# Three of the second product's seven products made by the seven-product scheme once more, from the third unit on

## The chip, the cores and the metric

The kernel runs on one core of a Trainium2 chip. The metric is the device time of one execution in microseconds (us). Where a kernel was compared closely, it was timed in turns with the kernel before on the same chip. TensorE multiplies, VectorE does elementwise work and empties PSUM (the memory, in banks, into which the matmuls add up), ScalarE does activations and copies, and DMA queues move data between DRAM and SBUF (the memory from which the engines take their operands). The granted clock is the share of TensorE's full speed that the profile records.

## The reference, cut to what matters

```python
kv  = np.einsum('bhsd,bhse->bhde', k, v)          # linear attention: (8, 8, 576, 64)
out = np.einsum('bhsd,bhde->bhse', q, kv)
x   = out / sqrt(mean(out*out, -1) + 1e-6) * g_norm   # then (4608, 512)
h   = x @ w_in                                    # 512 -> 2048   "first product"
g   = s * maximum(h, 0)**2 + b
return g @ w_out                                  # 2048 -> 512   "second product"
```

Everything is fp32.

## The kernel before

The 4608 rows are taken in nine units of 512. From the second unit on, the first and the second product of a unit are each made by a Strassen-Winograd scheme: seven products of half-sized blocks in place of eight. For the second product one of the seven is 256 rows x 1024 x 256; it runs as two row halves `j`, each eight matmuls of 128x128 by 128x256. The products are made in the order 1, 2, 6, 7, 5, 3, 4. Products 1, 6, 5 and 3 add up in one PSUM bank per half, and 7 and 4 in another. VectorE reads the bank between them.

```python
def product(i, j, ps, first):
    w2 = W2_AT[i] if u == 0 else ring[u, i]        # operand of w_out, a 1 MB tile fetched from DRAM
    for f in range(FC // 2):                       # 8 matmuls, contraction 128 each
        s, b = divmod(f, 2)
        matmul(ps, ga[G_OF[i], s][:, b, j*P : j*P+P], w2[:, f, :],
               first and f == 0, f == FC // 2 - 1)

def scaled(o, ps, other):                          # VectorE: o = s * ps + other, an "eviction"
    nc.vector.scalar_tensor_tensor(o, ps, s_col, other, ALU.mult, ALU.add)

return [lambda: x1(0), seq(lambda: x1(1), nxt(2), s2),   # s2: a11 = s1 - a11, operand of product 6
        lambda: z2(0), seq(lambda: z2(1), nxt(3), s4),   # s4: a12 = a12 - a11, operand of product 3
        lambda: x6(0), ...                               # (cut)
```

Between these steps stands the attention of the next unit's four chunks, by step number (`side`): `turn` transposes q on VectorE, `product` multiplies on TensorE and then squares (ScalarE), reduces and normalises (VectorE), `turn_x` transposes the result on VectorE, and ScalarE then scales it in pairs. The order is fixed by hand: in the traces below VectorE and ScalarE run their instructions in the order in which the program writes them (on VectorE of the changed kernel an eviction at 417.70, four subtractions from 418.10, the next eviction at 420.50; on ScalarE of e4 a scaling that waited 5.33 us at 437.66, and only then a square at 439.27).

## Time and profile before

| | before |
|---|---|
| time, median of the first 3 runs | 972.84 us (972.73 to 973.84) |
| span of the profiled run | 970.5 us |
| TensorE / VectorE / ScalarE busy | 99% / 50% / 20% |
| one unit | 104 us, of which 56.6 us second product |
| granted TensorE clock, mean | 0.998 |

Busy time is the union of an engine's instructions. A matmul record's duration is a model and longer than the spacing of two records (381 ns against 216 ns for 256 columns), so costs are read from start to start. The lines themselves stand in the prediction.

### The profile page before, as it was taken

To read this page: it belongs to the slowest core of one execution; us is meant where nothing else is said; L and a number is where in the kernel's file an instruction comes from. 1 tells how busy PE (TensorE), PEld (TensorE's weight loads), DVE (VectorE), ACT (ScalarE), POOL (GpSimd) and SP (SyncE) were. 2 spreads that over 40 slices of the span, in tenths; PEclk is the share of its full clock that TensorE was granted. 3 is DMA by queue.
4 is the path that set the end of the run, shared out by engine and by line. 5 is a ranking of instruction groups with operands and counts; after the bars stand their busy time and mean duration, and the time that the engine had idled before them with its cause. 6 is when DMAs were issued, how large, how long until landed. Compare 5 with 4: busy or idle time off the path is not lost.

```text
span 970.5 us, 15215 instructions
## 1 busy us (share of the span) xinstructions
PE 958.3 (99%) x6430; PEld 832.7 (86%) x6430; DVE 488.7 (50%) x803; ACT 194.6 (20%) x366; POOL 6.7 (1%) x18
## 2 busy tenths in 40 slices
PE   7999999999999999999999999999999999999997
PEld 7888888888888888888888888888888888888886
DVE  2789766554445434544446434644455345444431
ACT  3673132112120112111211112011201111111100
POOL 2000000000000000000000000000000000000000
PEclk9999999999999999999999999999999999999999
DMA  9588737732463257132363256225213430422032
GB/s 255 192 296 248 247 88 205 164 107 88 130 129 125 87 146 154 58 133 69 94 154 131 74 132 154 87 96 146 64 44 131 134 85 23 151 66 109 1 130 86
DMA packets 106931, 121.59 MB, mean 125 GB/s; under 512 B 74352, under 2 KB 80752, under 8 KB 99568
## 3 DMA queue, kind: packets, MB, share of 16 engines
q1 hardware_dynamic: 103760, 118.85, 41.8%
q10 hardware_dynamic: 2784, 1.77, 0.8%
q8 instruction: 50, 0.82, 0.4%
q14 instruction: 17, 0.14, 0.0%
q0 software_dynamic: 320, 0.00, 0.0%
HBM read 103.81 MB, written 16.78 MB: 124 GB/s over the span
## 4 chain that ended last, share of the span: by engine, by line
PE 95%; DMA 2%; DVE 1%; ACT 1%; SPq 0%; issue 0%; ACTq 0%; DVEq 0%
PE x_ps L87 50%; PE y_ps L87 31%; PE z_ps L87 9%; PE x_ps L412 3%; PE kv_ps L350 2%; DMA w_raw<-in_moe_w_in_dram 1%; DMA kv_sb<-in_k_dram 1%; DMA w_sb<-w 1%; PE qT_ps L391 0%; DVE xn L431 0%; DVE xT L455 0%; ACT xT L461 0%; ACT w_raw L206 0%; SPq L649 0%; DVE o L630 0%
## 5 line engine op out<-in xcount | busy, mean ns | idle before, releaser
L87 PE MATMUL x_ps<-w_sb,a 128*128 128x256 f32 x768 | 172.4, 381 | 0.0
L87 PEld LDWEIGHTS x_ps<-w_sb,a 128*128 128x128 f32 x768 | 145.0, 190 | 21.7 <-issue 2.8
L87 PE MATMUL y_ps<-w_sb,a 128*128 128x256 f32 x640 | 142.9, 381 | 1.4 <-DMA w_sb<-w 1.4
L87 PEld LDWEIGHTS y_ps<-w_sb,a 128*128 128x128 f32 x640 | 121.0, 190 | 19.1 <-DMA w_sb<-w 1.8
L87 PE MATMUL x_ps<-xs,ws 128*128 128x256 f32 x512 | 121.0, 379 | 0.0
L87 PE MATMUL y_ps<-xs,wb 128*128 128x256 f32 x512 | 121.0, 379 | 0.0
L557 ACT COPY r<-x_ps 128x512 f32<-128x512 f32 x96 | 56.2, 585 | 295.7 <-PE x_ps L87 289.0
L87 PEld LDWEIGHTS y_ps<-xs,wb 128*128 128x128 f32 x512 | 97.4, 190 | 13.1
L87 PEld LDWEIGHTS x_ps<-xs,ws 128*128 128x128 f32 x512 | 97.4, 190 | 13.1
L226 DVE TENSOR_TENSOR a<-y_ps,r 128x512 f32<-128x512 f32 x64 | 43.9, 686 | 122.3 <-ACT r L557 122.3
L87 PE MATMUL x_ps<-xT,wa 128*128 128x256 f32 x384 | 89.6, 380 | 0.1
L87 PEld LDWEIGHTS x_ps<-xT,wa 128*128 128x128 f32 x384 | 72.9, 190 | 10.4 <-ACT xT L461 0.5
L514 DVE SCALAR_TENSOR_TENSOR a<-a 128x512 f32<-128x512 f32 x96 | 66.4, 692 | 3.3
L630 DVE SCALAR_TENSOR_TENSOR or<-x_ps,s_col,b_row 128x256 f32<-128x256 f32 x52 | 25.0, 482 | 75.1 <-PE x_ps L87 73.2
L87 PE MATMUL x_ps<-xT,ws 128*128 128x256 f32 x256 | 61.1, 382 | 0.0
L87 PE MATMUL z_ps<-xT,wa 128*128 128x256 f32 x256 | 60.5, 379 | 0.0
L590 DVE TENSOR_TENSOR a<-a 128x512 f32<-128x512 f32 x32 | 22.1, 692 | 76.0 <-ACT a L589 76.0
L421 ACT ACTIVATE xn<-x_ps 128x512 f32<-128x512 f32 x34 | 20.3, 597 | 190.2 <-PE x_ps L412 187.8
L87 PE MATMUL x_ps<-w_sb,s 128*128 128x256 f32 x256 | 57.3, 382 | 0.0
L87 PEld LDWEIGHTS x_ps<-w_sb,s 128*128 128x128 f32 x256 | 48.1, 190 | 7.6 <-issue 1.4
L87 PEld LDWEIGHTS z_ps<-xT,wa 128*128 128x128 f32 x256 | 48.7, 190 | 6.6
L87 PEld LDWEIGHTS x_ps<-xT,ws 128*128 128x128 f32 x256 | 48.2, 190 | 6.6
(106 smaller groups left out, 821.1 us busy)
## 6 DMA issues: line engine op xcount, KB each, us to landing
w_sb<-w SPq DMA_DIRECT2D x56, 1024.0 KB, 5.0
kv_sb<-in_k_dram SPq DMA_DIRECT2D x30, 288.0 KB, 4.9
kv_sb<-in_v_dram SPq DMA_DIRECT2D x30, 288.0 KB, 5.8
w_raw<-in_moe_w_in_dram SPq DMA_DIRECT2D x8, 1024.0 KB, 7.6
w_raw<-in_moe_w_out_dram SPq DMA_DIRECT2D x8, 1024.0 KB, 5.2
out_dram<-o SPq DMA_DIRECT2D x104, 64.0 KB, 1.7
q_sb<-in_q_dram SPq DMA_DIRECT2D x144, 32.0 KB, 2.1
w<-w_up SPq DMA_DIRECT2D x3, 1024.0 KB, 8.0
```

The lines of the kernel that those rows point to most:

```text
L87: nc.tensor.matmul(o, lhsT=lhsT, rhs=rhs, start=start, stop=stop, skip_group_check=True)
L226: nc.vector.tensor_tensor(out=o, in0=a, in1=b, op=ALU.add)
L350: nc.tensor.matmul(ps[r][l * HB : l * HB + HB, i, :], lhsT=kv[rows, 0, l, j, :], rhs=kv[rows, 1, l, j, :], start=(j == 0), stop=(j == R - 1),)
L412: nc.tensor.matmul(ps[32 * p : 32 * p + 32, w, :], lhsT=st["qT"][:, p, 32 * w : 32 * w + 32], rhs=bd_kv[(b if w < 2 else b1) % 2][:, p, :] ...
L421: nc.scalar.activation(st["xn"], st["x"], AF.Square)
L514: nc.vector.scalar_tensor_tensor(t, t, 0.0, t, ALU.max, ALU.mult)
L557: nc.scalar.copy(st[name], src)
L590: nc.vector.tensor_mul(t, t, t)
L630: nc.vector.scalar_tensor_tensor(o, ps, s_col, other, ALU.mult, ALU.add)
```

## The change

Its intent is to save another eighth of the matmul time in products 2, 7 and 4. From the third unit on, such a product of 256 x 1024 x 256 is itself cut into quarters and made of seven products of 128 x 512 x 128. Each is four matmuls of 128x128 by 128x128. Below, products 2, 7 and 4 made so are the first, second and third *scheme product*, and m1 to m7 are the *quarter products* of one of them. A *half product* is one row half of a product made as before. An *eviction* is the VectorE instruction that reads a result out of PSUM. The operands that this needs of `w_out` are made in the second unit and kept in DRAM (`w3_dram`). Those of the activations are four VectorE sums per product. The diff, cut to its core:

```diff
+    TWICE = (2, 7, 4)
+    w3_dram = {i: dram.tile([P, 7, FC // 4, P], FP32, name=f"w3_{i}") for i in TWICE}
...
+        def parts_of_w(i):                       # second unit: 4 subtractions, 7 stores
...
+        def second_level(i, other, to):
+            def sums():
+                x11, x12, x21, x22 = (quarter(j, h) for j in range(2) for h in range(2))
+                add(s1, x21, x22); sub(s2, s1, x11); sub(s3, x11, x21); sub(s4, x12, s2)
+            def go(m, bank, first):
+                for f in range(FC // 4):
+                    matmul(t[bank], a[m][:, f], w[:, f], first and f == 0, f == FC // 4 - 1)
+            def keep(name, j, q):
+                scaled(r[name], t["x"], other(j, cols[q]))
+            def m1(): go(1, "x", True);  keep("r1", 0, 0)
+            def m2(): go(2, "z", True);  scaled(to(0, cols[0]), t["z"], r["r1"])
+            def m6(): go(6, "x", False); keep("r2", 1, 0)
+            def m7(): go(7, "y", True)
+            def m5(): go(5, "x", False); keep("r4", 1, 1); scaled(to(1, cols[1]), t["y"], r["r4"])
...                                               # m3 adds into "x", m4 into "y"
         return [
             lambda: x1(0),
-            seq(lambda: x1(1), nxt(2), s2),
-            lambda: z2(0),
-            seq(lambda: z2(1), nxt(3), s4),
...
+            seq(p2["sums"], lambda: x1(1), lambda: pump(2), s2),
+            seq(lambda: run(p2, 1, 2, 6, 7), lambda: pump(2)),
+            seq(p2[5], lambda: x6_of(0)),
+            seq(lambda: run(p2, 3, 4), lambda: pump(2), p7["sums"]),
+            seq(lambda: x6_of(1), lambda: pump(2), s4),
+            seq(lambda: run(p7, 1, 2, 6, 7), lambda: pump(2)),
+            seq(p7[5], lambda: x5_of(0)),
+            seq(p7[3], lambda: with_7(0), p7[4], lambda: pump(2)),
+            seq(lambda: x5_of(1), lambda: with_7(1), lambda: pump(2), p4["sums"]),
+            lambda: x3(0),
+            seq(lambda: run(p4, 1, 2, 6, 7, 5), lambda: pump(2)),
...
-        late["ring"] = ctx.enter_context(tc.tile_pool(name="ringp", bufs=3, side="right"))
+        late["ring"] = ctx.enter_context(tc.tile_pool(name="ringp", bufs=7, side="right"))  # half tiles
```

`pump(2)` fetches the next two half tiles of operands. The `side` table of the attention is unchanged.

More of the change, by code (lines that the diff above doesn't have):

```diff
@@ L270 @@
     w2_dram = [dram.tile([P, FC // 2, HN], FP32, name=f"w2_{i}") for i in range(8)]
+    TWICE = (2, 7, 4)
+    w3_dram = {
+        i: dram.tile([P, 7, FC // 4, P], FP32, name=f"w3_{i}") for i in TWICE
+    }
     w_up = convp.tile([P, FC // 2, DM], FP32, name="w_up")
@@ L322 @@
     b_row = const.tile([P, DM], FP32, name="b_row")
+    b_12 = const.tile([P, HN], FP32, name="b_12")
     def bias_row():
@@ L329, in bias_row @@
         nc.scalar.copy(b_row, ps)
+        sub(b_12, b_row[:, :HN], b_row[:, HN:])
     def warm(n):
@@ L495, in x_of @@
         return xs[u, i][:, c, :]
-    ga = {}
+    ga, g_pair = {}, {}
     bank = {}
@@ L516, in g_tile @@
     def g_tile(name, s):
-        ga[name, s] = gp.tile([P, 2, TB], FP32, name=name, tag=name)
+        if s % 2 == 0:
+            g_pair[name, s // 2] = gp.tile([P, 2, 2, TB], FP32, name=name, tag=name)
+        ga[name, s] = g_pair[name, s // 2][:, s % 2]
         return ga[name, s]
@@ L606, with twice, pump @@
     late = {}
-    def load_w2(u, n):
-        t = late["ring"].tile([P, FC // 2, HN], FP32, name="w2_sb", tag="w2")
-        nc.sync.dma_start(out=t, in_=w2_dram[ORDER[n]])
-        ring[u, ORDER[n]] = t
+    def twice(u, i):
+        return u > 1 and i in TWICE
+    queue_w2 = [
+        (u, i, n) for u in range(1, U) for i in ORDER for n in range(4 if twice(u, i) else 2)
+    ]
+    def pump(k):
+        for u, i, n in queue_w2[:k]:
+            t = late["ring"].tile([P, 4 * HN], FP32, name="w2_sb", tag="w2")
+            if twice(u, i):
+                t = t.rearrange("p (m f n) -> p m f n", m=2, n=P)
+                k2 = min(2, 7 - 2 * n)
+                nc.sync.dma_start(out=t[:, :k2], in_=w3_dram[i][:, 2 * n : 2 * n + k2])
+            else:
+                t = t.rearrange("p (f n) -> p f n", n=HN)
+                nc.sync.dma_start(out=t, in_=w2_dram[i][:, 4 * n : 4 * n + 4])
+            ring[u, i, n] = t
+        del queue_w2[:k]
     out_9 = out.rearrange("(b p j) n -> b j p n", p=HB, j=R)
@@ L620, in product @@
         def product(i, j, ps, first):
-            w2 = W2_AT[i] if u == 0 else ring[u, i]
             for f in range(FC // 2):
                 s, b = divmod(f, 2)
+                w2 = W2_AT[i][:, f] if u == 0 else ring[u, i, f // 4][:, f % 4]
                 matmul(
-                    ps, ga[G_OF[i], s][:, b, j * P : j * P + P], w2[:, f, :],
+                    ps, ga[G_OF[i], s][:, b, j * P : j * P + P], w2,
                     first and f == 0, f == FC // 2 - 1,
@@ L632, in mm2 @@
         b1, b2 = b_row[:, :HN], b_row[:, HN:]
+        def parts_of_w(i):
+            y = [[ring[u, i, n][:, :, q * P : q * P + P] for q in range(2)] for n in range(2)]
+            (y11, y12), (y21, y22) = y
+            t1, t2, t3, t4 = (
+                late["sub"].tile([P, FC // 4, P], FP32, name="sub", tag="sub") for _ in range(4)
+            )
+            sub(t1, y12, y11)
+            sub(t2, y22, t1)
+            sub(t3, y22, y12)
+            sub(t4, y21, t2)
+            for n, t in enumerate((y11, y21, t2, t3, t1, y22, t4)):
+                nc.sync.dma_start(out=w3_dram[i][:, n], in_=t)
@@ new lines, in second_level, with quarter, m1, m2 @@
+        def second_level(i, other, to):
+            a, t, r = {}, {}, {}
+            cols = [slice(q * P, q * P + P) for q in range(2)]
+            def quarter(j, h):
+                g = g_pair[G_OF[i], h].rearrange("p s b t -> p (s b) t")
+                return g[:, :, j * P : j * P + P]
+            def sums():
+                x11, x12, x21, x22 = (quarter(j, h) for j in range(2) for h in range(2))
+                s1, s2, s3, s4 = (
+                    late["sub"].tile([P, FC // 4, P], FP32, name="sub", tag="sub")
+                    for _ in range(4)
+                )
+                add(s1, x21, x22)
+                sub(s2, s1, x11)
+                sub(s3, x11, x21)
+                sub(s4, x12, s2)
+                a.update({1: x11, 2: x12, 3: s4, 4: x22, 5: s1, 6: s2, 7: s3})
+            def go(m, bank, first):
+                if first:
+                    t[bank] = bank_of((bank, i), "z" if bank == "z" else "y", 1 if bank == "z" else 2)
+                    t[bank] = t[bank].rearrange("p b n -> p (b n)")[:, :P]
+                n = ORDER.index(m)
+                w = ring[u, i, n // 2][:, n % 2]
+                for f in range(FC // 4):
+                    matmul(t[bank], a[m][:, f], w[:, f], first and f == 0, f == FC // 4 - 1)
+            def keep(name, j, q):
+                r[name] = late["tmp"].tile([P, P], FP32, name="r", tag="r")
+                scaled(r[name], t["x"], other(j, cols[q]))
+            def m1():
+                go(1, "x", True)
+                keep("r1", 0, 0)
+            def m2():
+                go(2, "z", True)
+                scaled(to(0, cols[0]), t["z"], r["r1"])
+            def m6():
+                go(6, "x", False)
+                keep("r2", 1, 0)
+            def m7():
+                go(7, "y", True)
+            def m5():
+                go(5, "x", False)
+                keep("r4", 1, 1)
+                scaled(to(1, cols[1]), t["y"], r["r4"])
+            def m3():
+                go(3, "x", False)
+                scaled(to(0, cols[1]), t["x"], other(0, cols[1]))
+            def m4():
+                go(4, "y", False)
+                scaled(to(1, cols[0]), t["y"], r["r2"])
+            return {"sums": sums, 1: m1, 2: m2, 6: m6, 7: m7, 5: m5, 3: m3, 4: m4}
@@ L732, in seq @@
             return run
-        def nxt(n):
-            if n >= 7:
-                return (lambda: load_w2(u + 1, n - 7)) if u + 1 < U else (lambda: None)
-            return lambda: load_w2(u, n)
         def t3():
@@ L765, in mm2 @@
             ]
+        if u == 1:
+            return [
+                lambda: x1(0),
+                seq(lambda: x1(1), lambda: pump(2), s2),
+                seq(lambda: z2(0), lambda: parts_of_w(2)),
+                seq(lambda: z2(1), lambda: pump(2), s4),
+                lambda: x6(0),
+                seq(lambda: x6(1), lambda: pump(2)),
+                seq(lambda: y7(0), lambda: parts_of_w(7)),
+                seq(lambda: y7(1), lambda: pump(2)),
+                lambda: x5(0),
+                seq(lambda: x5(1), lambda: pump(2)),
+                lambda: x3(0),
+                seq(lambda: x3(1), lambda: pump(2)),
+                seq(lambda: y4(0), lambda: parts_of_w(4)),
+                seq(lambda: y4(1), lambda: pump(2)),
+            ]
@@ new lines, in mm2, with x6_of, x5_of, with_7 @@
+        p2 = second_level(2, lambda j, q: st["r1", j][:, q], lambda j, q: rows("o1", j)[:, q])
+        p7 = second_level(
+            7, lambda j, q: b2[:, q], lambda j, q: rows("o2", j)[:, HN:][:, q]
+        )
+        p4 = second_level(4, lambda j, q: st["r2", j][:, q], lambda j, q: rows("o2", j)[:, q])
+        def x6_of(j):
+            product(6, j, st["x", j], False)
+            part("r2", j, st["x", j], b_12)
+        def x5_of(j):
+            product(5, j, st["x", j], False)
+        def with_7(j):
+            right = st["o2", j][:, HN:]
+            add(st["r2", j], st["r2", j], right)
+            scaled(right, st["x", j], right)
+            if last(j):
+                store("o2", j, 4 * u + 2 + j, slice(HN, DM))
@@ L766, in mm2, with y4_of, run @@
+        def y4_of(j, m):
+            p4[m]()
+            if last(j):
+                store("o2", j, 4 * u + 2 + j, slice(0, HN), (nc.sync, nc.scalar))
+            else:
+                store("o2", j, 4 * u + 2 + j)
+        def run(steps, *which):
+            for m in which:
+                steps[m]()
         return [
             lambda: x1(0),
-            seq(lambda: x1(1), nxt(2), s2),
-            lambda: z2(0),
-            seq(lambda: z2(1), nxt(3), s4),
-            lambda: x6(0),
@@ L772, in mm2 @@
-            seq(lambda: x6(1), nxt(4)),
-            lambda: y7(0),
-            seq(lambda: y7(1), nxt(5)),
-            lambda: x5(0),
-            seq(lambda: x5(1), nxt(6)),
+            seq(p2["sums"], lambda: x1(1), lambda: pump(2), s2),
[4 more added lines that the diff above has]
+            seq(lambda: run(p7, 1, 2, 6, 7), lambda: pump(2)),
@@ L777, in mm2 @@
+            seq(p7[5], lambda: x5_of(0)),
+            seq(p7[3], lambda: with_7(0), p7[4], lambda: pump(2)),
+            seq(lambda: x5_of(1), lambda: with_7(1), lambda: pump(2), p4["sums"]),
             lambda: x3(0),
-            lambda: x3(1),
-            lambda: y4(0),
-            lambda: y4(1),
+            seq(lambda: run(p4, 1, 2, 6, 7, 5), lambda: pump(2)),
+            seq(lambda: x3(1), lambda: pump(2)),
+            seq(lambda: y4_of(0, 3), lambda: y4_of(1, 4), lambda: pump(2)),
@@ L787, in tc_late @@
         convp.release()
-        late["ring"] = ctx.enter_context(tc.tile_pool(name="ringp", bufs=3, side="right"))
+        late["ring"] = ctx.enter_context(tc.tile_pool(name="ringp", bufs=7, side="right"))
+        late["sub"] = ctx.enter_context(tc.tile_pool(name="subp", bufs=5, side="right"))
+        late["tmp"] = ctx.enter_context(tc.tile_pool(name="tmpp", bufs=4, side="right"))
         late["kv"] = ctx.enter_context(tc.tile_pool(name="kvp", bufs=2, side="right"))
@@ L840 @@
     kv0p.release()
-    gp = ctx.enter_context(tc.tile_pool(name="gp", bufs=NS))
+    gp = ctx.enter_context(tc.tile_pool(name="gp", bufs=NS // 2))
     turn, product, norm, turn_x, take = zip(*(attention(c, True) for c in range(4)))
@@ L988 @@
                 load_kv(kv_due[1], i, late["kv"], tag="kv")
-        if u + 1 < U:
-            load_w2(u + 1, 0)
-            load_w2(u + 1, 1)
+            pump(7)
 _INS = ['q', 'k', 'v', 'g_norm', 'moe_w_in', 'moe_w_out', 'moe_s', 'moe_b']
```

## The prediction

> **What bounds the kernel now.** I read the page first, then the waits, then the order of time inside one unit, and last the only matmuls of the width that the change brings in.
>
> ```profile
> PE 958.3 (99%) x6430; PEld 832.7 (86%) x6430; DVE 488.7 (50%) x803; ACT 194.6 (20%) x366; POOL 6.7 (1%) x18
> ...
> PE 95%; DMA 2%; DVE 1%; ACT 1%; SPq 0%; issue 0%; ACTq 0%; DVEq 0%
> ...
> L87 PE MATMUL x_ps<-w_sb,a 128*128 128x256 f32 x768 | 172.4, 381 | 0.0
> ```
>
> The first line is the busy time of each engine, the second the chain that ended last, the third the costliest group. TensorE is 99% busy, the chain is 95% TensorE, and the large group never sat idle. So TensorE work is the time, and a change pays only by taking matmul time away without opening gaps. VectorE is at 50%, which says it has room on average and nothing about any one moment.
>
> The chain in order of time shows a product of the second matrix product (both row halves, 32 records of 256 columns) at 6.91 us, that is 0.2158 us a record; an fp32 matmul leaves two records. The mean of 381 ns in the group is no cost: records overlap. Units repeat every 104 us; in the unit I read, the second product runs from 605.88 to 662.51 us, 56.6 us.
>
> The change needs the same figure for 128 columns with a new 128x128 stationary operand each time. The attention of the first chunks has just that (timeline, TensorE alone; columns: start us, us from first start to last end, engine, line, operation, operands, count):
>
> ```profile
> 16.90 1.06 PE L87 MATMUL y_ps<-bd_kv,qT 128*128 128x128 f32 x8
> 17.79 0.39 PE L87 MATMUL warm_ps<-ident 128*128 128x128 f32 x2
> ```
>
> Eight records go from 16.90 to the next start at 17.79: 0.89/8 = 0.1113 us each, at full clock. That is 0.516 of 0.2158, so halving the columns nearly halves the cost, and the weight load (about 190 ns a record in both widths) does not set it.
>
> Next is the order of VectorE work as the second product starts, in the same unit:
>
> ```profile
> 612.79 3.62 PE L87 MATMUL x_ps<-w_sb,a 128*128 128x256 f32 x16
> ...
> 613.95 0.68 DVE L226 TENSOR_TENSOR a<-y_ps,r 128x512 f32<-128x512 f32 x1
> 614.67 0.69 DVE L514 SCALAR_TENSOR_TENSOR a<-a 128x512 f32<-128x512 f32 x1
> 616.24 3.62 PE L87 MATMUL z_ps<-w_sb,a 128*128 128x256 f32 x16
> 616.44 0.48 DVE L630 SCALAR_TENSOR_TENSOR or<-x_ps,s_col,b_row 128x256 f32<-128x256 f32 x1 [1.08 <-PE x_ps L87]
> 616.84 2.49 DVE L229 TENSOR_TENSOR a<-s,a 128x512 f32<-128x512 f32 x4
> ```
>
> The reader should see that VectorE follows program order: the eviction of product 1's second half waits for its last matmul (616.44), then come the four subtractions that make the next operand (2.49 us, 0.61 us start to start). None of this holds TensorE now, because the product that adds into the same PSUM bank starts 6.9 us later. There are only 1.1 us of slack in front of 616.44.
>
> [...] this trace drops to half clock for 3.4 us after the start-up gaps of 0.85 and 1.02 us around 20 to 22 us, and never again.
>
> **The change part by part.**
> *Removed and added on TensorE.* A product of 32 records at 0.2158 (6.91 us) becomes seven of eight records at 0.1113 (0.89 us each, 6.23 us). Gain 0.68 us a product; three products in each of seven units: 21 x 0.68 = 14.2 us.
> *Added on VectorE, per unit.* Twelve sums of 128x512 (0.61 to 0.72 us start to start) and 21 evictions of 128x128. VectorE reads of PSUM take 0.482 us for 256 columns (row of or on x_ps) and 0.684 for 512 (row of a on z_ps); continued downward that is 0.38 us for 128, an estimate. About 8 + 8 us, less four removed evictions (1.9): +14 us, in seven units 98 us, plus 8 us for the twelve subtractions of the second unit. VectorE goes to about 595 us. It stays under TensorE.
> *Moved, on the path.* Inside the new scheme the first, third, fifth and sixth quarter products accumulate in one bank. m1 is evicted before m6 may add, and only m2 (0.89 us) lies between. From m1's start its eviction ends after 0.78 (last of 8 starts) + 0.28 (record) + 0.38 = 1.44 us, against 1.78 for m1 and m2. So VectorE may be 0.34 us late; anything more is a gap on TensorE. In the diff the program order ahead of those evictions is crowded:
> - First scheme product: the four sums stand ahead of the eviction of product 1's second half. They start at 615.4 (after the square at 614.67) and let the next instruction start at 617.95; that eviction takes 0.4, four subtractions 2.45, so m1's eviction runs 620.8 to 621.2. m6 could have started at 616.24 + 1.78 = 618.0. Gap 3.2 us. Without the sums it would still be 1.5.
> - Second scheme product: its four sums stand ahead of the transpose for the next chunk's attention, whose matmuls TensorE meets first: gap 1.4 us. Those matmuls' reduction and normalisation, and four more subtractions plus a transpose, stand ahead of m1's eviction. Walking the queue from the previous normalisation's multiply (0.61, 2 x 0.3, 2.55, 0.6, 0.4, 2.4, 0.7, then the 2.1 us from reduction to multiply that the trace shows, then 0.6 and 0.38) it ends 4.7 us after m1's start; 1.8 is hidden. Gap 2.9 us.
> - Third scheme product: sums, a transpose and a normalisation delay it too, but a 3.45 us half product lies before it: gap 0.6 us.
> Sum per unit 8.1 us, six units 48.6. The last unit has no attention: 3.2 + 1.7 = 4.9. Its wait of 1.41 us for the last weight tile (row of waits of y_ps on w_sb) should go, since seven half tiles are fetched ahead.
> *Traffic.* Twenty half-megabyte tiles a unit instead of fourteen: +3 MB in 104 us, beside 125 GB/s on average and slices of 296. Hidden.
> Sum: 972.8 - 14.2 + 48.6 + 4.9 - 1.4 = 1010.7. I add 3 us for the second unit's stores and a few windows at half clock: 1014.
>
> **The rivals.**
> *(a) The gain arrives whole*: VectorE is only half busy and the new order hides its work. Then 959 us. For it: the average; half products were placed between the steps. Against: the queue above, in which m1's eviction stands behind work that cannot start before product 1 ends.
> *(b) Weight loads bind* at 128 columns in a long stream: at 0.2158 x 16/28 = 0.1233 us a record the gain is gone, about 973 without gaps. Against: 16 records at 0.111.
> *(c) Half clock*: gaps near 3 us may cost up to 1.7 us of lost work each. With two such gaps in seven units up to 24 us more, 1035. For it: the drop at 22 us. [...]
> *(d) Half the gaps*: if sums start earlier or the walk double counts, only 3.2 and about 1.5 per unit remain: about 992.
>
> **Range and chances.** (d) and (c) give the ends of the range, 988 to 1034. Slower by 2% begins at 992.3; only (a), (b) or a strongly softened (d) stay under it. Faster by 2% would need 953.4, more than the whole gain of 14.2.
>
> **What would show it.** Records of 128x128 at about 0.111 us start to start; TensorE idle of 3 us ahead of m6 of the first and second scheme product, released by an eviction at VectorE; TensorE busy time falling by some 14 us while its share falls to about 94%; about 1.4 us before the second chunk's attention matmuls, released by the transpose; VectorE about 595 us. I am wrong if the group of new matmuls shows next to no idle time, if the spacing is above 0.12 us, or if the waits are on weight tiles.

In the trace before, the clock was granted at 0.50 for 3.41 us from 22.09. The 1.7 us of (c) are half of that, an estimate. The sum is 972.8 - 14.2 + 48.6 + 4.9 - 1.4 = 1010.7, and 1014 with the 3 us on top, an allowance of mine that was not worked out from a trace. That an accumulation waits for the eviction of its bank was not shown by the trace before; the result shows it (36.7 us below).

## The result

| | before | changed |
|---|---|---|
| median | 972.79 us (4 runs) | 1019.42 us (4 runs) |
| range | 970.95 to 973.84 | 1010.50 to 1023.51 |
| span of the profiled run | 970.5 us | 1015.7 us |
| granted clock, mean, of the changed kernel's runs | | 0.980 to 0.994 |

The changed kernel is slower: ratio 1.0469, 95% interval 1.0395 to 1.0543. Two things meet the eye. The time rose by 46 us, and the runs scatter over 13 us where those of before scatter over 3.

The page of the changed kernel, the line of busy times, and, from its groups by form (line, engine, operation, operands, shapes, count, then busy us, mean ns, idle us before them and its releaser), the two groups that waited:

```profile
PE 959.4 (94%) x6934; PEld 847.5 (83%) x6934; DVE 580.0 (57%) x1019; ACT 194.8 (19%) x366; POOL 6.7 (1%) x18
```

```profile
L90 PE MATMUL y_ps<-w_sb,sub 128*128 128x128 f32 x672 | 95.6, 302 | 36.7 <-DVE r L659 36.7
...
L421 PE MATMUL x_ps<-bd_kv,qT 128*32 128x128 f32 x1056 | 35.7, 275 | 7.7 <-DVE qT L391 6.8 <-DVE xn L440 0.5 <-DVE qT L407 0.3
```

TensorE fell from 99% to 94% of a longer span. The new matmuls, those that read a sum, waited 36.7 us in total, all of it for the eviction `r` on VectorE. The attention's matmuls waited 6.8 us for the transposed q. In the kernel before the first group did not exist and the second had waited 0.5 us:

```profile
L412 PE MATMUL x_ps<-bd_kv,qT 128*32 128x128 f32 x1056 | 36.0, 278 | 0.5 <-DVE xn L431 0.5
```

(The chain that ended last is of no use in this profile: it could be followed back over only 2% of the span. Waits and groups tell what it does not.)

One unit of each in windows (us from the start of the span; then length, and busy us of TensorE, weight loads, VectorE, ScalarE, GpSimd; granted clock, DMA share, GB/s). Before:

```profile
605.88:662.51 56.63, 56.63 (x369) 48.59 (x368) 29.39 (x52) 8.18 (x18) 0.00 (x0) 1.00 0.27 89
```

Changed, the fourth unit, which had no window at half clock:

```profile
405.65:467.56 61.91, 55.41 (x442) 49.30 (x440) 39.69 (x78) 8.19 (x18) 0.00 (x0) 1.00 0.42 133
```

The stretch of the second product grew by 5.3 us. TensorE was idle for 6.5 us of it, and VectorE took on 10.3 us. The order of time in the same unit shows the first of the gaps:

```profile
412.56 3.62 PE L90 MATMUL x_ps<-w_sb,a 128*128 128x256 f32 x16
...
415.17 0.69 DVE L229 TENSOR_TENSOR sub<-a,a 128x512 f32<-128x512 f32 x1
...
416.01 1.05 PE L90 MATMUL y_ps<-w_sb,a 128*128 128x128 f32 x8
...
416.90 1.06 PE L90 MATMUL z_ps<-w_sb,a 128*128 128x128 f32 x8
417.10 0.68 DVE L232 TENSOR_TENSOR sub<-a,sub 128x512 f32<-128x512 f32 x1
417.70 0.48 DVE L659 SCALAR_TENSOR_TENSOR or<-x_ps,s_col,b_row 128x256 f32<-128x256 f32 x1
418.10 2.49 DVE L232 TENSOR_TENSOR a<-s,a 128x512 f32<-128x512 f32 x4
420.50 0.35 DVE L659 SCALAR_TENSOR_TENSOR r<-y_ps,s_col,or 128x128 f32<-128x128 f32 x1
420.90 2.95 PE L90 MATMUL y_ps<-w_sb,sub 128*128 128x128 f32 x24 [2.94 <-DVE r L659]
```

The first quarter product starts at 416.01 and the second at 416.90. The third could start at 417.79, but it adds into the bank of the first, whose eviction runs only at 420.50. Ahead of that eviction VectorE did the four sums (415.17 to 417.70), the eviction of product 1's second half, and the four subtractions for product 6 (418.10). TensorE started again 0.05 us after the eviction ended.

I measured every gap as the distance of two matmul starts less the usual spacing (0.22 us for 256 columns, 0.115 for 128). In each unit from the third on there is one of 3.1 us there, one of 1.29 before the second chunk's attention and one of 2.59 at the same place of the second scheme product; in the last unit 3.1 and 1.62. The third scheme product has 0.04. The sum of those over 0.3 us is 6 x (3.1 + 1.29 + 2.59) + 3.1 + 1.6 = 46.6 us.

The gaps bring something else. Here are two windows of 3.4 us from the third unit (the columns are as above):

```profile
306.40:309.82 3.42, 1.44 (x13) 1.44 (x13) 2.52 (x6) 0.00 (x0) 0.00 (x0) 1.00 0.67 213
309.82:313.23 3.41, 3.41 (x17) 3.23 (x16) 1.39 (x4) 0.00 (x0) 0.00 (x0) 0.50 0.38 86
```

In the first, TensorE was busy for 1.44 of 3.42 us; in the next, the clock was granted at half (0.50). This happened seven times in the profiled run (an eighth such stretch begins after the last matmul and costs no work). At a clock of 0.50 half the work of 3.41 us is lost each time, by my estimate: 7 x 1.7 = 11.9 us. The account of the span is then 970.5 - 14.0 (matmul time saved) - 1.4 (the last weight tile, no longer waited for) + 46.6 + 11.9 = 1013.6 us, against 1015.7.

### The profile page after: what moved, and what is told of

It is laid out like the page before. It is cut to its first block, busy times and chain, and to the rows that moved or that the text cites. A ratio compares the mean times of both kernels' runs of the same rounds, so it can differ in the third digit from the quotient of the medians.

```text
span 1015.7 us, 16743 instructions
## 1 busy us (share of the span) xinstructions
PE 959.4 (94%) x6934; PEld 847.5 (83%) x6934; DVE 580.0 (57%) x1019; ACT 194.8 (19%) x366; POOL 6.7 (1%) x18
## 3 DMA queue, kind: packets, MB, share of 16 engines
q1 hardware_dynamic: 124352, 140.88, 48.6%
HBM read 120.33 MB, written 22.28 MB: 140 GB/s over the span
## 5 line engine op out<-in xcount | busy, mean ns | idle before, releaser
L90 PE MATMUL x_ps<-w_sb,a 128*128 128x256 f32 x768 | 175.1, 382 | 0.0
L90 PE MATMUL y_ps<-w_sb,sub 128*128 128x128 f32 x672 | 95.6, 302 | 36.7 <-DVE r L659 36.7
L90 PEld LDWEIGHTS y_ps<-w_sb,sub 128*128 128x128 f32 x672 | 89.2, 213 | 42.5 <-DVE r L659 39.3
L90 PE MATMUL y_ps<-w_sb,a 128*128 128x128 f32 (+1 forms) x416 | 62.8, 297 | 0.0
L90 PEld LDWEIGHTS y_ps<-w_sb,a 128*128 128x128 f32 x416 | 57.1, 191 | 4.1 <-issue 1.4
```

What stands on the lines that cost most here:

```text
L90: nc.tensor.matmul(o, lhsT=lhsT, rhs=rhs, start=start, stop=stop, skip_group_check=True)
```

## The experiments

The theory: the saved matmul time is real, and the whole loss is TensorE standing still because VectorE's program order puts other work ahead of the eviction that frees the bank, plus the half clock that these gaps bring. The rivals: the scheme itself costs (128-column matmuls, VectorE's load, DMA traffic); the wait is for an operand or a weight tile and not for the eviction; the half clock has another cause.

**Filling the gaps, e1_fill.** Idle matmuls into an unused bank stand where the gaps were.

```diff
             def m6():
+                fill({2: 13, 7: 11 if u + 1 < U else 6, 4: 0}[i])   # 128x128 matmuls of the identity
                 go(6, "x", False)
...
-            seq(lambda: x6_of(1), lambda: pump(2), s4),
+            seq(lambda: x6_of(1), lambda: fill(5 if u + 1 < U else 0), lambda: pump(2), s4),
```

> Only the gaps are filled: 13 idle matmuls of 128 columns (0.22 us each, 2.9 us) before m6 of the first scheme product, 11 before m6 of the second, 5 before the second chunk's attention, into an unused PSUM bank. Nothing that VectorE does moves, so the same evictions end the same waits. Theory (the half-clock windows of the changed kernel, and its scatter of 13 us, come from TensorE being idle in them): no half-clock window after the start-up, granted clock 0.998, all runs within 1.5 us of each other, and 972.8 - 14.2 + 46.6 - 1.4 = 1004 us (46.6 is the sum of the gaps seen). Rival (the half clock comes from something else, such as the 128-column matmuls themselves [...]): clock still 0.98 to 0.994, scatter of 10 us, about 1016 to 1020 us.

Measured: 1006.77 us (1006.36 to 1008.77, 4 runs), ratio 1.036 to before. The clock came out as expected:

```profile
die 0 (median of its cores): 1003.9 us, clock 0.999
```

No half-clock window is left between start and end, and the scatter is 2.4 us instead of 13 (1.5 was expected, and the median is 3 us above the 1004 expected). Nothing was made faster except the clock, and the profiled span fell from 1015.7 to 1003.9 us, by 11.8; the seven windows were put at 11.9. The gaps cause the half clock, and the gaps themselves are the larger part of the loss.

**Only the first gap, e2_first_gap.** The subtractions for product 6 go behind the second eviction.

```diff
-            seq(p2["sums"], lambda: x1(1), lambda: pump(2), s2),
-            seq(lambda: run(p2, 1, 2, 6, 7), lambda: pump(2)),
+            seq(p2["sums"], lambda: x1(1), lambda: pump(2)),
+            seq(lambda: run(p2, 1, 2, 6), s2, p2[7], lambda: pump(2)),
```

> Only one thing moves: the four subtractions that make the operand of product 6 go from behind product 1 to behind the second eviction of the first scheme product. Same instructions, same data. Theory (m6 waits for m1's eviction, which stands behind those subtractions in VectorE's order): the first gap falls from 3.1 to about 0.7 us in each of seven units (the four sums still end 0.7 us late), so 17 us less idle time; the other gaps stay at 1.3 and 2.6; 987 us at full clock, 987 to 994 with some half-clock windows. Rival (m6 waits for its operand, the sum, or for its weight tile): the gap stays near 3.1 us and the time near 1017.

Measured: 998.23 us (996.33 to 999.53, 4 runs), ratio 1.0266. The gap fell from 3.1 to 0.70 us in every unit, the figure expected, and the other two stayed at 1.28 and 2.59. The time is 4 us above the range that I gave. The account as above, with these gaps (29.7 us) and the four half-clock windows of its profiled run (6.8 us; mean granted clock 0.992), gives a span of 991.6 us against 995.5. About 2 us of the rest is common to all kernels with the whole scheme (the changed kernel 2.1, e1 2.2, e7 1.7), and most of that lies at the end: from the end of the last matmul record to the end of the span they take 5.7 us, the kernel before 4.0. What is left, some 2 us in e2, I did not trace. The group that waits, in the groups by form:

```profile
L90 PE MATMUL y_ps<-w_sb,sub 128*128 128x128 f32 x672 | 91.3, 293 | 19.8 <-DVE r L659 19.8
```

So m6 waited for the eviction and not for its operand, which was made at the same moment as before (its first sum 0.85 us ahead of m1 in both), nor for a weight tile.

**Only the sums split, e8_sums_split (one look, state unknown).** Of the first scheme product's four sums two stay in front and two go behind m1's eviction.

```diff
                 add(s1, x21, x22)
                 sub(s2, s1, x11)
-                sub(s3, x11, x21)
-                sub(s4, x12, s2)
+                if i != 2: sub(s3, x11, x21); sub(s4, x12, s2)
...
                 keep("r1", 0, 0)
+                if i == 2: ...                    # the two sums here
```

> Only the first scheme product's four sums change: two stay ahead of product 1's second half, two go behind m1's eviction; the subtractions for product 6 stay in front of it. Theory (the queue in front of m1's eviction is a plain sum): the first gap shrinks by two sums, 1.2 us, from 3.1 to 1.9; the other gaps stay. Rival (the subtractions alone set it, and they start when product 1 ends, whatever stands before): the gap stays near 3.1.

Measured: the gap is 1.90 us in each unit, and the one run took 1006.89 us. The group that waits, in the groups by form:

```profile
L90 PE MATMUL y_ps<-w_sb,sub 128*128 128x128 f32 x672 | 92.9, 296 | 28.2 <-DVE r L659 28.2
```

From 36.7 to 28.2 is 8.5 us, seven units of 1.2: two VectorE instructions of 0.61 us each. The queue in front of the eviction is a plain sum.

**Only the surroundings of the second scheme product, e3_second_gaps.**

```diff
-            seq(lambda: run(p2, 3, 4), lambda: pump(2), p7["sums"]),
-            seq(lambda: x6_of(1), lambda: pump(2), s4),
+            seq(lambda: run(p2, 3, 4), lambda: pump(2)),
+            seq(p7["sums"], lambda: x6_of(1), lambda: pump(2)),
             seq(lambda: run(p7, 1, 2, 6, 7), lambda: pump(2)),
-            seq(p7[5], lambda: x5_of(0)),
+            seq(p7[5], s4, lambda: x5_of(0)),
...
+        if u > 0:
+            side[5] = []
+            side[6] = [turn_x[0], product[1], turn[2]]
```

> Only the surroundings of the second scheme product move: its four sums go behind the transpose of the second chunk, the four subtractions for product 3 go behind its fourth eviction, and the attention of the second chunk goes behind its fourth quarter product. Theory: the gaps of 1.3 and 2.6 us go to 0 to 0.2 in six units, that of 1.6 in the last unit too, so 25 us less idle; the first gap of 3.1 stays; 979 us at full clock, 979 to 986 with half-clock windows. Rival (VectorE has too much work in this stretch whatever its order, 57% busy on average but more here): the waits move to other matmuls and the time stays above 1000.

Measured: 1012.82 us (1010.37 to 1015.12, 4 runs), ratio 1.0417. This is a miss. The two gaps that it aimed at went, but a new one of 2.74 us came in each of six units, at the attention of the fourth chunk:

```profile
L421 PE MATMUL x_ps<-bd_kv,qT 128*32 128x128 f32 x1056 | 36.2, 279 | 16.2 <-DVE qT L391 15.6 <-DVE xn L440 0.5
```

And the first gap still cast its half-clock windows (mean granted clock 0.983). By this run alone the rival, that VectorE has too much to do here whatever its order, stood as well as my theory.

**Both, e4_both.** e2 and e3 together, and the sums of the first scheme product split as in e8.

> Both moves, and the first scheme product's sums in two pairs, the second behind m1's eviction. Matmuls, VectorE instructions, tiles and bytes are those of the changed kernel; only the order differs. Theory (the matmul saving of 14 us is real and the whole loss is order and the half clock it brings): no gap over 0.3 us in the later units, no half-clock window, 958 us, 1.5% under the kernel before. Rival (the scheme itself costs: long streams of 128-column matmuls, more VectorE work, 3 MB more a unit): above 973.

Measured: 980.10 us (978.98 to 987.12, 6 runs), ratio 1.0091 (1.0066 to 1.0116). Above 973, so it counts for the rival. Its trace says otherwise. The group with the sums no longer waits, and what remains is the gap of e3, with the four half-clock windows of this run (mean granted clock 0.993):

```profile
L90 PE MATMUL y_ps<-w_sb,sub 128*128 128x128 f32 x672 | 85.5, 279 | 0.0
...
L421 PE MATMUL x_ps<-bd_kv,qT 128*32 128x128 f32 x1056 | 37.9, 287 | 16.5 <-DVE qT L391 15.7 <-DVE xn L440 0.5 <-DVE qT L407 0.3
```

In the order of time of its fourth unit:

```profile
434.52 2.48 DVE L232 TENSOR_TENSOR a<-a,a 128x512 f32<-128x512 f32 x4
435.09 1.08 PE L421 MATMUL x_ps<-bd_kv,qT 128*32 128x128 f32 x32
...
436.92 0.70 DVE L464 STREAM_TRANSPOSE xT<-xn 128x512 f32<-128x512 f32 x1
...
437.66 1.70 ACT L470 ACTIVATE xT<-xT,g_col 128x256 f32<-128x256 f32 x4 [5.33 <-DVE xT L464]
...
439.27 0.57 ACT L430 ACTIVATE xn<-x_ps 128x512 f32<-128x512 f32 x1
439.88 0.69 DVE L432 TENSOR_REDUCE ss<-xn 128x8 f32<-128x512 f32 x1 [2.25 <-ACT xn L430]
...
443.34 0.70 DVE L391 STREAM_TRANSPOSE qT<-q_sb 128x512 f32<-128x512 f32 x1
...
444.19 1.58 PE L421 MATMUL x_ps<-bd_kv,qT 128*32 128x128 f32 x32 [2.58 <-DVE qT L391]
```

The third chunk's product was done at about 436, but its square on ScalarE came at 439.27, behind the scaling of an earlier block, which had waited for a VectorE transpose, which I had put behind the four subtractions. VectorE then stood idle for 2.25 us waiting for that square, with the transpose that TensorE needed (443.34) further back in its own queue. VectorE was idle while it was the bound: a matter of order, not of load.

**The third order, e7_order.** That transpose goes in front, the subtractions go where VectorE was idle, and the third scheme product's sums are split too.

```diff
+            seq(lambda: run(p7, 1, 2, 6, 7), lambda: pump(2), lambda: s4((0, 1))),
+            seq(p7[5], lambda: s4((2, 3)), lambda: x5_of(0)),
...
+            side[7] = [turn[3], product[2], turn_x[1]]
+            side[8] = []
```

(on top of e4; the sums of product 4 split like those of product 2)

> The third order. In the previous one the eviction gaps went but a new one of 2.74 us came: the transpose of the fourth chunk stood behind the third chunk's normalisation, whose square on ScalarE waited for the scaling of the first pair's transposed block, which waited for a VectorE transpose behind the four subtractions for product 3. Here that transpose goes ahead of the third chunk's product, the block's transpose behind it, the four subtractions are made two and two where VectorE was idle, and the third scheme product's sums are split as the first one's. Same instructions. Theory (everything lost is order and the half clock it brings): no gap over 0.3 us in the units from the third on, no half-clock window, 958 to 960 us, 1.4% under the kernel before. Rival (VectorE's work cannot be fitted in this stretch): again 2 to 3 us gaps at another matmul, 970 or more.

Measured: correct, 960.19 us (958.68 to 961.76, 4 runs), ratio 0.9881 (0.9866 to 0.9897). It is faster than both kernels, 1.2% under the one before. (e4, e7 and e9: that they differ from the kernel before rests on their intervals, which exclude 1.) The page's busy times, and the same two groups:

```profile
PE 943.5 (99%) x6934; PEld 835.4 (87%) x6934; DVE 578.7 (60%) x1019; ACT 194.7 (20%) x366; POOL 6.7 (1%) x18
```

```profile
L90 PE MATMUL y_ps<-w_sb,sub 128*128 128x128 f32 x672 | 85.3, 279 | 0.0
...
L421 PE MATMUL x_ps<-bd_kv,qT 128*32 128x128 f32 x1056 | 35.7, 276 | 0.9 <-DVE xn L440 0.5 <-DVE qT L407 0.3
```

Against the changed kernel it has the same 6934 matmuls and loads, the same 1019 VectorE instructions and the same tiles. Waiting fell from 36.7 to 0.0 us, and TensorE is at 99% of a span of 956.8 us. No gap over 0.11 us is left in the matrix products of the later units, and no half-clock window before the end (TensorE busy for 61.00 of 61.00 us from 409 to 470; mean granted clock 0.998). One cost of the scheme as such shows, the longer end: its last matmul record ends at 951.1 of 956.8 us, that of the kernel before at 966.6 of 970.5, which is 1.7 us more. The order cost 59 us.

**Product 4 alone, e5_only_4.** Products 2 and 7 are made as before.

```diff
-    TWICE = (2, 7, 4)
+    TWICE = (4,)
...                                # the steps of the kernel before up to x5(1), then p4["sums"]
```

> One part alone: only the third scheme product (product 4) is made by the scheme, products 2 and 7 as before; the ring of seven half tiles and the prepared operands of product 4 stay. In the changed kernel this one had no gap, since a half product lies between its sums and its first eviction. Theory (the matmul saving is real, the loss is gaps at products 2 and 7): 7 x 0.68 = 4.8 us less matmul time and 1.4 us less waiting for the last weight tile, no gaps, full clock: 966 to 967 us. Rival (the scheme costs as such): 973 or more, rising by a third of the changed kernel's 46 us to about 987.

Measured: 971.39 us (970.61 to 971.90, 5 runs), and a wrong result by my mistake. In the kernel before, products 7 and 4 add up in one bank; I split them and left 7 out. As a timing it is nearly the intended kernel. Its eviction gap of 0.55 us in six units, 3.3 us in all, explains most of the missing gain of 5 us.

**The same, mended, e9_only_4_right.** Product 7 is added to what product 4's evictions read, and product 4's sums are split.

```diff
+            elif u > 1:
+                scaled(st["r2", j], st["y", j], st["r2", j])     # in y7
```

> The run with product 4 alone, mended: product 7 is now added where product 4 needs it (one eviction of 256 columns more per half), and product 4's last two sums go behind its first eviction. The earlier one, wrong in its result because product 7 was left out of a bank that it no longer shared, had gaps of 0.55 us in six units (3.3 us) that ate most of its gain. Theory: no gap over 0.2 us, so 7 x 0.68 = 4.8 us and 1.4 us less than before: 966 to 967.5 us, ratio 0.994. Rival (something beside the gaps ate the gain of product 4): again 971 us.

Measured: correct, 966.70 us (965.91 to 968.44, 6 runs), ratio 0.9946 (0.9934 to 0.9959), with no such gap. One of the three products, made without gaps, yields its share.

**The prepared operands alone, e6_prepared_only.** The second unit makes and stores the operands, and the ring has seven half tiles, but no product uses the scheme.

```diff
         def twice(u, i):
-            return u > 1 and i in TWICE
+            return False
```

(and all later units take the second unit's steps, without its preparation)

> The other parts alone: the second unit still makes and stores the operands (12 subtractions, 21 stores), the ring has seven half tiles, but all units multiply as before. Theory: nothing of this is on TensorE's path; the wait for the last weight tile (1.4 us) goes: 971.0 to 972.8 us. Rival (the stores of the second unit or the half tiles cost): 975 or more, with waits on weight tiles.

Measured: 971.13 us (970.27 to 973.04, 5 runs), ratio 0.9991 (0.9977 to 1.0004). No cost of the preparation and the smaller tiles shows. The wait for the last weight tile (1.4 us in the kernel before) is gone from the trace. The interval, 2.2 us faster to 0.4 slower, holds both its 1.4 us and no gain at all, so a cost of about that size could hide in it.

## Why the prediction was right

The predicted time was 1014, the range 988 to 1034; measured were 1019.4, and slower by 4.7%.

- *The matmul saving* was put at 0.1113 us a record and 14.2 us in all. In the changed kernel eight records go from 416.01 to 416.90, 0.89 us, as read from the kernel before. e7 confirms the sum to 2 us: it lies 12 us under before, and its span 14 under that of before, where 15.6 with the last weight tile was expected. One sign failed: TensorE's busy time was to fall by some 14 us, and it rose from 958.3 to 959.4. It counts the work at half clock at its stretched length, about 12 us; in e7, without half clock, it is 943.5.
- *The first gap* was predicted at 3.2 us and measured at 3.1. Its parts were right as well: e2 left 0.70 of it by moving the subtractions, e8 left 1.9 by moving two sums. (That 1.5 would be left without any sums ahead is a slip: the prediction's own figures, 616.44 + 0.4 + 2.45 + 0.38 against 618.0, give 1.7. No run tried it.)
- *The second scheme product* was predicted at 1.4 and 2.9, measured at 1.29 and 2.59; in the last unit 1.7 and 1.62. One entry of the walk was misread: from reduction to multiply the trace before shows 1.36 us (633.13 to 634.49), not 2.1. The entries add up to 10.9 us and measured 9.95 (430.37 to 440.32); as the gap still came out within 0.3 us, another part of the walk must have been off the other way, so this agreement is partly luck.
- *The third* was predicted at 0.6 and measured at 0.04. The walk there was too coarse: m1's eviction ended just in time (459.14 plus 0.34, against a start at 459.54).
- *The sum of the gaps* was 53.5 predicted, 46.6 measured. The half clock went the other way: I allowed 3 us, for it and the stores of the second unit, and called up to 24 a rival; it took 11.9 in the profiled run. No cost of the stores showed (e6). This term was mis-sized: my ground for so little was that the gaps were too short for it, which no trace had shown. Gaps of 2.6 to 3.1 us were enough when most of one fell into one window (1.93 to 2.81 us idle of 3.41). The trace before had already shown this: its half clock at 22 us followed a window with 1.87 us of idle TensorE, from gaps of 0.85 and 1.02 us. The two errors nearly cancel, 7 us too much and 9 us too little; that 1014 came so near to 1019 is luck in part, the mechanism is not.
- *VectorE* came to 580 us, not 595: an eviction of 128 columns takes 0.35 us and not 0.38, some 4 us for 147 of them. For the rest, consecutive instructions overlap in the union that busy time is (430.98 and 431.24 in the fourth unit start 0.26 us apart and last 0.34); this I did not add up.
- *The rivals.* That the gain arrives whole (959) was the wrong forecast for this kernel and the right one for its mended order (960). That weight loads bind is excluded by the spacing (0.111 us a record, where 0.123 was needed). That gaps come out at half (992) did not happen; with the figures given for it this case adds up to 990, and the stated range begins at 988. The extra traffic was 2.4 MB a unit and not 3 (HBM read 120.33 MB against 103.81 in seven units); no wait on a weight tile came of it in e7.

## What to carry to other kernels

An accumulation that alternates between engines in one PSUM bank has a deadline: here the eviction had 0.34 us to spare, because only one quarter product of 0.89 us lay between. Before shrinking matmuls on a TensorE-bound kernel, list what stands ahead of each such eviction in the program order of the engine that makes it (here two sums cost 1.2 us, e8, and four subtractions 2.4 us, e2), including work that itself waits for TensorE or ScalarE; a mean of 50% busy says nothing about it. If a scheme that should pay loses, change the order before giving up the scheme: the same instructions gave 1019 and 960 us.

## What the traces show of the half clock and of an eviction

- The half clock came after idle TensorE, and gaps of 2.6 to 3.1 us did it. In the changed kernel's profiled run seven windows of 3.41 us with 1.93 to 2.81 us of idle TensorE were each followed by half clock (0.50) for 3.41 us before the last matmul, and none with 1.89 us or less was; in the kernel before, one with 1.87 us was, at the start-up (18.68 to 22.09). So these two traces give no one limit. Gaps of the same length did it in some units and not in others: the first gap is 3.1 us in all seven, and the window that holds most of it had 1.97 us idle at 306.40 (half clock followed) and 1.86 at 419.04 (none). This also makes run times scatter (13 us against 2.4 in e1, where the gaps were filled).
- The spacing from an eviction to the next instruction is shorter than the eviction's record: 0.26 us for 128 columns (from 430.98 to 431.24 in the changed kernel) against 344 to 351 ns, and 0.40 for 256 (from 616.44 to 616.84 in the one before) against about 481. In the gap above TensorE started only after the end of the eviction's record (420.90 after 420.85), so there the longer figure counts.
- With nothing ahead of it that held it up, an eviction ended 1.45 us after the start of a quarter product of 0.89 us (in e7: matmuls from 405.58, eviction 406.68 to 407.03), 0.34 us before the next one into its bank started (407.37).
